# Query features of the last batch one per unit, and two more down chunks in exact parts

## The chip, the cores and the metric

The kernel runs on one core of a Trainium2 chip. The metric is device time in microseconds (us) of one execution. The core has five instruction queues that run side by side and wait for each other by semaphores: TensorE (PE, with its weight loads shown apart as PEld), VectorE (DVE), ScalarE (ACT), GpSimd (POOL) and SyncE (SP, which here only issues DMAs). SBUF is the on-chip memory of the engines, PSUM the memory that TensorE accumulates into[...].

## The reference

Two stages, one after the other: a linear attention with polynomial features, then a gated feed-forward block on its output.

```python
# q, k, v: (4, 4, 1088, 32); S1, S2: (8, 32)
def phi(x):
    a = einsum('rd,bhsd->bhsr', S1, x)
    b = einsum('rd,bhsd->bhsr', S2, x)
    return einsum('bhsi,bhsj->bhsij', a, b).reshape(..., 64)
q_p, k_p = phi(q), phi(k)
kv = einsum('bhsf,bhsd->bhfd', k_p, v)
z = sum(k_p, axis=2)
attn = einsum('bhsf,bhfd->bhsd', q_p, kv) / (einsum('bhsf,bhf->bhs', q_p, z) + 1e-6)

x = attn.transpose(0, 2, 1, 3).reshape(4352, 128)
g = x @ w_gate                       # (128, 1536)
out = (g * sigmoid(g) * (x @ w_val)) @ w_out   # (1536, 128)
```

All inputs and outputs are float32.

## The kernel before

The feed-forward work is cut into token blocks. Three small blocks come from the first batch; then come the *later blocks* (the list `line`), six of 480 tokens and a last one of 384. The hidden dimension of 1536 is cut into 12 chunks of 128. One block and one chunk make a **unit**; the main loop over `y` (the last `for y in range(END)`) runs 7 x 12 = 84 units in order, so the first later block is units 0 to 11, the third one (`line[2]`) units 24 to 35.

A unit works in two halves, and the halves of neighbouring units overlap. In step `y`, `start_unit` of unit y+1 runs first: two matmuls (L990) into the gate bank and the value bank of a pair of PSUM banks, which ScalarE then rescales in place (L993). Then `finish_unit` of unit y adds four matmuls (L1002, L1003). These are float32 products done as three fast products of cut-down operands ("parts"). ScalarE applies Silu to the gate bank into `sg` (L1005), and VectorE multiplies by the value bank into `hbuf` (L1010). There are three pairs of banks, so unit y+3 reuses unit y's pair: its first L990 overwrites the gate bank, read last by L1005, its second L990 the value bank, read last by L1010.

After that comes `down`, the product of a finished chunk with `w_out`. The list `todo` holds five chunks, so the chunk of unit y-5 is taken in step y. It is done in one of two ways. A *plain* chunk is one full float32 matmul (L1078), two instructions in the trace. A chunk in the list `DOWN` is done in *exact parts*: three fast matmuls (L1070, L1072, L1073) on parts of the hidden values, which `cut_hidden` makes for it. The three parts are made by three engines. The first (`h1`) comes one unit later, on ScalarE (L969, put behind the unit's other work in `behind`) or on VectorE (L967, put ahead of it in `before`). The second (`h0 = h - h1`) comes two units later on GpSimd (L970), the third (`hd`) three units later on VectorE (L973). `cut_hidden` rotates over six sets of three buffers. In the third later block the chunks 2, 4, 6, 8, 9 and 10 are in `DOWN`, all six with `h1` on ScalarE; in the fourth, chunks 1, 2, 4, 5, 7, 8, 9, 10, and in the fifth and sixth chunk 6 too, with `h1` of 2, 5, 8 and 10 on VectorE.

Tokens of the next block are cut into parts by `cut_tokens`: first part on ScalarE (L865), second on GpSimd (L868), third on VectorE (L873). For the fourth later block this takes place at units 27 and 32.

Between these units the attention of batches 1 to 3 advances. It is a generator (`attentions`), and `parts_of(n)` takes n steps of it. In units below 20 one step is taken in each unit, from 20 on only in even ones. At the units in `GROUPS` (4, 6, 20, 22, 40) `group` runs it up to the next step that holds many matmuls. Of batch 3, the last, the group at unit 22 makes the query sketches; then come eight steps of `query_step`: the denominators (L741, L744), their reciprocal (L746 to L748), and three times a feature product (L377) and a transposition (L758). After that nothing is left but the group at unit 40, whose numerators (`numerators`, L776) multiply the transposed features by the key-value sums.

Down weights are cut by `cut_down` in units 20 to 29 on ScalarE (L915, L923, L932) and GpSimd (L918, L926).

The order on each engine is written out by hand (the schedule is manual): instructions run on each engine in the order in which these functions emit them, and `now(before, y)` and `now(behind, y)` emit the pieces that were set aside for unit y.

Of the kernel before, what the change touches and what calls it, by code (L numbers as in the profile page):

```python
# [19 lines left out]
def kernel(  # L20
# [796 lines left out]
    def whole(ap):  # L817
        return ap.bitcast(FP32)
# [66 lines left out]

    line = list(range(HEAD, len(blocks)))
    FINE, PLAIN = range(1, NCH - 1), [0, 1, 3, 5, 7, 6, NCH - 1]
    DOWN = [(line[2], j) for j in (2, 4, 6, 8, 9, 10)]
    DOWN += [(i, j) for i in line[3:6] for j in (1, 2, 4, 5, 7, 8, 9, 10)]
    DOWN += [(i, 6) for i in line[4:6]]  # L890
    DOWN += [(LAST, j) for j in (1, 2, 4, 5, 6, 7)]
    down_parts = {}
# [4 lines left out]
    def add_to(where, y, f):  # L897
        where.setdefault(y, []).append(f)

    def now(where, y):  # L900
        for f in where.pop(y, ()):
            f()
# [49 lines left out]
    def cut_hidden(y, i, j):  # L952

        if not h_sets:
            x = []
            for tag in ("kld", "qld", "vld", "kT", "qT"):
                t = const.tile([P, 2, WB], F32R, tag=tag, name="h" + tag, bufs=1)
                x += [t[:, k, :] for k in range(2)]
            t = const.tile([P, 8, WB], F32R, tag="late", name="hlate", bufs=1)
            x += [t[:, k, :] for k in range(8)]  # L960
            h_sets.extend(x[k : k + 3] for k in range(0, 18, 3))
        n = SPLIT if i == LAST else blocks[i][1]
        h_sets.append(h_sets.pop(0))
        h1, h0, hd = h_parts[i, j] = [x[:, 0:n] for x in h_sets[-1]]
        h = hidden[i, j][:, 0:n]
        if j in (2, 5, 8, 10) and i != line[2]:
            add_to(before, y + 1, lambda: nc.vector.tensor_scalar(h1, h, CUT, None, op0=ALU.mult))  # L967
        else:
            add_to(behind, y + 1, lambda: nc.scalar.activation(h1, h, AF.Copy, scale=CUT))  # L969
        add_to(before, y + 2, lambda: nc.gpsimd.tensor_tensor(  # L970
            out=h0, in0=h, in1=whole(h1), op=ALU.subtract
        ))
        add_to(before, y + 3, lambda: nc.vector.scalar_tensor_tensor(  # L973
            out=hd, in0=whole(h1), scalar=WHOLE, in1=h, op0=ALU.mult, op1=ALU.subtract
        ))
# [8 lines left out]
    def start_unit(i, j):  # L984

        n = blocks[i][1]
        xd = x_parts[i][2][:, 0:n]
        ps = sums_of[i, j] = pair((i, j))[:, :, 0:n]
        for k, w in enumerate((wg, wv)):
            nc.tensor.matmul(  # L990
                ps[:, k], w_parts[id(w), j // 3][2][:, j % 3, :], xd, start=True, stop=True
            )
        nc.scalar.activation(ps, ps, AF.Copy, scale=-1.0 / WHOLE)  # L993

    def finish_unit(i, j, y=None):
        n = blocks[i][1]
        x1, x0, _ = (x[:, 0:n] for x in x_parts[i])
        ps = sums_of.pop((i, j))
        now(before, y)
        for k, w in enumerate((wg, wv)):  # L1000
            w1, wb = (w_parts[id(w), j // 3][t][:, j % 3, :] for t in range(2))
            nc.tensor.matmul(ps[:, k], w1, x1, start=False, stop=False, skip_group_check=True)  # L1002
            nc.tensor.matmul(ps[:, k], wb, x0, start=False, stop=True, skip_group_check=True)  # L1003
        sg = fpool.tile([P, WB], FP32, tag="sg", name="sg", bufs=5)[:, 0:n]
        nc.scalar.activation(sg, ps[:, 0], AF.Silu, scale=WHOLE)  # L1005
        slot_of[i, j] = slots.pop(0)
        hj = slot_of[i, j]
        hidden[i, j] = hj
        todo.append((i, j))
        nc.vector.scalar_tensor_tensor(  # L1010
            out=hj[:, 0:n], in0=ps[:, 1], scalar=WHOLE, in1=sg, op0=ALU.mult, op1=ALU.mult
        )
        let_go((i, j))
        now(behind, y)
        if (i, j) in DOWN:
            cut_hidden(y, i, j)
# [38 lines left out]
    def down(y=None):  # L1055

        i, j = todo.pop(0)
        n = SPLIT if i == LAST else blocks[i][1]
        first = i not in acc
        if first:  # L1060
            acc[i] = bank("g2" if i == 1 or i in line[2::2] else "acc")
        made[i] = made.get(i, 0) + 1
        mine = [c for c in range(NCH) if (i, c) in DOWN]
        if mine and j == mine[0]:
            acc[i, "p"] = bank("acc" if i in line[2::2] else "g2")
        sides = dict(start=first, stop=(made[i] == NCH))
        if j in mine:
            w1, wb, wd = [down_parts[x][:, FINE.index(j), :] for x in ("w1", "wb", "wd")]
            h1, h0, hd = h_parts.pop((i, j))
            nc.tensor.matmul(acc[i][:, 0:n], wd, hd, **sides)  # L1070
            p = acc[i, "p"][:, 0:n]
            nc.tensor.matmul(p, w1, h1, start=(j == mine[0]), stop=False)  # L1072
            nc.tensor.matmul(p, wb, h0, start=False, stop=(j == mine[-1]))  # L1073
            if j == mine[-1]:
                copy_out(y, i, n)
        else:
            w = down_parts["scaled"][:, PLAIN.index(j), :] if mine else wo[:, j, :]
            nc.tensor.matmul(acc[i][:, 0:n], w, hidden[i, j][:, 0:n], **sides)  # L1078
        if i != LAST:
            hidden.pop((i, j))  # L1080
            slots.append(slot_of[i, j])
        if made[i] == NCH:
            if mine:
                put_together(y, i, n)
            elif i == HEAD - 1:

                add_to(behind, 1, lambda: store(i, n))
            else:
                store(i, n)
# [163 lines left out]
    def parts_of(n):  # L1253

        for _ in range(n):
            if ahead[0] not in ("pe", "end"):
                ahead[0] = next(att, "end")

    def group():
        while ahead[0] != "pe":  # L1260
            ahead[0] = next(att)
        ahead[0] = next(att, "end")
# [132 lines left out]
    slots[:] = [flat[:, WB * k : WB * k + WB] for k in range((NH - NL) * BW // WB)]  # L1395

    END = len(line) * NCH
    GROUPS, WIDE, EASY = (4, 6, 20, 22, 40), (20, 40), 20

    token_steps = {}  # L1400
    for m, i in enumerate(line[1:], 1):
# [4 lines left out]
    for y in range(END):  # L1406
        if y in GROUPS:
            group()
        at = [(line[x // NCH], x % NCH) for x in (y, y + 1) if x < END]
        if y in WIDE:  # L1410
            finish_unit(*at[0], y)
        if y + 1 < END:
            start_unit(*at[1])
        if y not in WIDE:
            finish_unit(*at[0], y)
        for _ in range(2):

            if len(todo) > min(5 + (todo[0] == (line[1], 0)), END - y + 1):
                down(y)
        parts_of(y < EASY or y % 2 == 0)  # L1420
        for gen in token_steps.get(y, ()):
            next(gen, None)
        if y in range(20, 30):
            next(down_steps, None)
# [43 lines left out]
```

## Time and profile before

| | us |
|---|---|
| median of three runs | 276.89 |
| lowest and highest | 276.75, 277.1 |
| the profiled execution | 276.78 |
| its span, first to last instruction | 275.0 |

Busy time in four stretches of the span (us; the first holds units 23 to 28, the next units 29 to 34, then 35 to 39, and the group at unit 40):

| stretch | length | TensorE | VectorE | ScalarE | GpSimd |
|---|---|---|---|---|---|
| 145.7 to 158.4 | 12.70 | 12.70 | 7.97 | 11.35 | 4.69 |
| 158.4 to 170.8 | 12.40 | 12.40 | 8.99 | 11.05 | 5.35 |
| 170.8 to 180.9 | 10.10 | 10.10 | 8.30 | 8.66 | 4.11 |
| 180.9 to 184.8 | 3.90 | 3.82 | 2.24 | 1.61 | 2.01 |

The profile names engines and lines: "DVE L1010" is the VectorE instruction of line 1010. In the timeline each line has the start in us from the span's beginning, the duration, engine, line, operation, output and input names with their shapes, a count, and in brackets how long the engine had stood idle and whom it waited for. The granted TensorE clock was 1.000 throughout. A matmul's duration in the trace includes its time in the pipeline, so the pace of TensorE is read from the distance between starts.

### The profile page before, as it was taken

To read this page: it belongs to the slowest core of one execution; us is meant where nothing else is said; L and a number is where in the kernel's file an instruction comes from. 1 tells how busy PE (TensorE), PEld (TensorE's weight loads), DVE (VectorE), ACT (ScalarE), POOL (GpSimd) and SP (SyncE) were. 2 spreads that over 40 slices of the span, in tenths; PEclk is the share of its full clock that TensorE was granted. 3 is DMA by queue.
4 is the path that set the end of the run, shared out by engine and by line. 5 is a ranking of instruction groups with operands and counts; after the bars stand their busy time and mean duration, and the time that the engine had idled before them with its cause. 6 is when DMAs were issued, how large, how long until landed. Compare 5 with 4: busy or idle time off the path is not lost.

```text
span 275.0 us, 5775 instructions
## 1 busy us (share of the span) xinstructions
PE 269.2 (98%) x2189; PEld 200.3 (73%) x2189; DVE 212.5 (77%) x371; ACT 192.8 (70%) x347; POOL 103.5 (38%) x115
## 2 busy tenths in 40 slices
PE   8899999999999999999999999999999999999995
PEld 7545566666785787777577777867887888789994
DVE  3997988989798773887545666967977996998771
ACT  3468565472685686677479898769879888897880
POOL 3314422159250630260043353435335663553320
PEclk9999999999999999999999999999999999999999
DMA  6583196222231043000200020000100200010021
GB/s 192 170 228 83 43 278 190 68 97 70 54 92 21 1 115 95 2 0 0 38 13 4 4 36 0 0 2 11 26 2 0 36 1 0 14 24 1 5 33 29
DMA packets 26139, 14.30 MB, mean 52 GB/s; under 512 B 19840, under 2 KB 24192, under 8 KB 26112
## 3 DMA queue, kind: packets, MB, share of 16 engines
q1 hardware_dynamic: 25456, 13.84, 19.6%
q8 instruction: 17, 0.28, 0.4%
q10 hardware_dynamic: 656, 0.10, 0.2%
q14 instruction: 10, 0.08, 0.1%
HBM read 11.41 MB, written 2.23 MB: 50 GB/s over the span
## 4 chain that ended last, share of the span: by engine, by line
PE 93%; DVE 3%; DMA 2%; ACT 1%; issue 0%; SPq 0%
PE PS L1078 21%; PE PS L1002 14%; PE PS L990 14%; PE PS L1003 14%; PE PS L1026 12%; PE PS L1070 3%; PE PS L1073 3%; PE PS L1072 3%; PE PS L354 2%; PE PS L776 2%; PE PS L342 2%; PE PS L388 2%; DMA kld<-in_k_dram 2%; PE PS L1118 1%; PE PS L497 1%; PE PS L445 1%
## 5 line engine op out<-in xcount | busy, mean ns | idle before, releaser
L993 ACT ACTIVATE PS<-PS 128x960 f32<-128x960 f32 (+1 forms) x90 | 83.3, 926 | 30.6 <-PE PS L990 29.8
L1010 DVE SCALAR_TENSOR_TENSOR hbuf<-PS,sg 128x480 f32<-128x480 f32 (+1 forms) x87 | 55.2, 635 | 38.4 <-ACT sg L1005 35.4
L1005 ACT ACTIVATE sg<-PS 128x480 f32<-128x480 f32 (+1 forms) x90 | 49.6, 551 | 1.6 <-PE PS L1003 1.2
L1078 PE MATMUL PS<-hbuf,wo 128*128 128x480 f32 (+2 forms) x94 | 39.4, 516 | 0.0
L990 PE MATMUL PS<-xd,graw 128*128 128x480 f32 (+1 forms) x69 | 37.7, 546 | 0.0
L990 PE MATMUL PS<-xd,wd 128*128 128x480 f32 (+1 forms) x90 | 33.5, 372 | 0.0
L1003 PE MATMUL PS<-x,wb 128*128 128x480 f32 (+1 forms) x90 | 33.5, 372 | 0.0
L1002 PE MATMUL PS<-x,w 128*128 128x480 f32 (+1 forms) x90 | 33.4, 371 | 0.0
L1003 PE MATMUL PS<-x,graw 128*128 128x480 f32 (+1 forms) x69 | 25.5, 370 | 0.0
L990 PEld LDWEIGHTS PS<-xd,wd 128*128 128x128 f32 x90 | 17.0, 189 | 10.0 <-issue 5.5
L1026 PE MATMUL PS<-xT,wg 128*128 128x384 f32 (+1 forms) x60 | 23.5, 474 | 0.1
L1026 PE MATMUL PS<-xT,wv 128*128 128x384 f32 (+1 forms) x60 | 23.1, 467 | 0.3 <-DVE wv L286 0.3
L1078 PEld LDWEIGHTS PS<-hbuf,wo 128*128 128x128 f32 x94 | 17.6, 189 | 5.4 <-issue 0.4
L868 POOL TENSOR_TENSOR x<-xT,x 128x480 fp32r<-128x480 f32 (+1 forms) x6 | 7.2, 1193 | 38.0 <-ACT x L865 38.0
L1030 ACT ACTIVATE sg<-PS 128x384 f32<-128x384 f32 (+1 forms) x24 | 11.2, 468 | 13.2 <-PE PS L1026 12.4
L970 POOL TENSOR_TENSOR hlate<-hbuf,hlate 128x480 fp32r<-128x480 f32 (+1 forms) x12 | 14.3, 1188 | 14.2 <-ACT hlate L969 11.3
L1078 PE MATMUL PS<-hbuf,scaled 128*128 128x480 f32 (+1 forms) x44 | 18.7, 514 | 0.0
L990 PEld LDWEIGHTS PS<-xd,graw 128*128 128x128 f32 x69 | 13.0, 188 | 7.7 <-ACT PS L993 4.1
L1002 PEld LDWEIGHTS PS<-x,w 128*128 128x128 f32 x90 | 16.9, 188 | 2.2
L1003 PEld LDWEIGHTS PS<-x,wb 128*128 128x128 f32 x90 | 16.9, 188 | 2.1
L1002 PE MATMUL PS<-x,graw 128*128 128x480 f32 (+1 forms) x48 | 18.0, 376 | 0.0
L1026 PEld LDWEIGHTS PS<-xT,wv 128*128 128x128 f32 x60 | 11.2, 190 | 7.4 <-DVE hbuf L1041 0.8
(205 smaller groups left out, 565.1 us busy)
## 6 DMA issues: line engine op xcount, KB each, us to landing
kld<-in_k_dram SPq DMA_DIRECT2D x4, 544.0 KB, 4.2
vld<-in_v_dram SPq DMA_DIRECT2D x12, 144.0 KB, 4.0
qld<-in_q_dram SPq DMA_DIRECT2D x3, 544.0 KB, 4.0
raw<-in_moe_w_out_dram SPq DMA_DIRECT2D x4, 384.0 KB, 4.3
raw<-in_moe_w_gate_dram SPq DMA_DIRECT2D x3, 384.0 KB, 3.3
raw<-in_moe_w_val_dram SPq DMA_DIRECT2D x3, 384.0 KB, 3.6
out_dram<-o SPq DMA_DIRECT2D x16, 60.0 KB, 2.0
vld<-in_v_dram SPq DMA_DIRECT2D x4, 112.0 KB, 3.9
```

The lines of the kernel that those rows point to most:

```text
L970: add_to(before, y + 2, lambda: nc.gpsimd.tensor_tensor(out=h0, in0=h, in1=whole(h1), op=ALU.subtract))
L990: nc.tensor.matmul(ps[:, k], w_parts[id(w), j // 3][2][:, j % 3, :], xd, start=True, stop=True)
L993: nc.scalar.activation(ps, ps, AF.Copy, scale=-1.0 / WHOLE)
L1002: nc.tensor.matmul(ps[:, k], w1, x1, start=False, stop=False, skip_group_check=True)
L1003: nc.tensor.matmul(ps[:, k], wb, x0, start=False, stop=True, skip_group_check=True)
L1005: nc.scalar.activation(sg, ps[:, 0], AF.Silu, scale=WHOLE)
L1010: nc.vector.scalar_tensor_tensor(out=hj[:, 0:n], in0=ps[:, 1], scalar=WHOLE, in1=sg, op0=ALU.mult, op1=ALU.mult)
L1026: nc.tensor.matmul(o[:, 0:n], w[:, j, :], xT[:, t0 : t0 + n], start=True, stop=True)
L1030: nc.scalar.activation(sg[:, 0:n], g[:, 0:n], AF.Silu)
L1070: nc.tensor.matmul(acc[i][:, 0:n], wd, hd, **sides)
L1072: nc.tensor.matmul(p, w1, h1, start=(j == mine[0]), stop=False)
L1078: nc.tensor.matmul(acc[i][:, 0:n], w, hidden[i, j][:, 0:n], **sides)
```

## The change

It has three edits. The attention takes a step in every unit from 24 to 31 (`SOON`), where it took one in even units only. The last batch's six feature steps, which were in the even units 26 to 36, are then in units 25 to 30, one in each. In the third later block chunks 5 and 7 join `DOWN`: their down products are made of exact parts and no longer of one plain matmul, and their three parts are made by the engines named above. And in that block `h1` of chunks 5, 7 and 9 is on VectorE; chunks 2, 4, 6, 8 and 10 have it on ScalarE.

On VectorE this adds three L967 and two L973, on GpSimd two L970; ScalarE has one L969 less; on TensorE two L1078 matmuls are replaced by two each of L1070, L1072 and L1073. SP's list is the same.

```diff
@@
     line = list(range(HEAD, len(blocks)))
     FINE, PLAIN = range(1, NCH - 1), [0, 1, 3, 5, 7, 6, NCH - 1]
-    DOWN = [(line[2], j) for j in (2, 4, 6, 8, 9, 10)]
+    DOWN = [(line[2], j) for j in (2, 4, 5, 6, 7, 8, 9, 10)]
     DOWN += [(i, j) for i in line[3:6] for j in (1, 2, 4, 5, 7, 8, 9, 10)]
@@
         h = hidden[i, j][:, 0:n]
-        if j in (2, 5, 8, 10) and i != line[2]:
+        if j in ((5, 7, 9) if i == line[2] else (2, 5, 8, 10)):
             add_to(before, y + 1, lambda: nc.vector.tensor_scalar(h1, h, CUT, None, op0=ALU.mult))
         else:
             add_to(behind, y + 1, lambda: nc.scalar.activation(h1, h, AF.Copy, scale=CUT))
@@
     END = len(line) * NCH
-    GROUPS, WIDE, EASY = (4, 6, 20, 22, 40), (20, 40), 20
+    GROUPS, WIDE, EASY, SOON = (4, 6, 20, 22, 40), (20, 40), 20, range(24, 32)
@@
             if len(todo) > min(5 + (todo[0] == (line[1], 0)), END - y + 1):
                 down(y)
-        parts_of(y < EASY or y % 2 == 0)
+        parts_of(y < EASY or y % 2 == 0 or y in SOON)
         for gen in token_steps.get(y, ()):
             next(gen, None)
```

## The prediction

> **What bounds the kernel now.** I read the page's busy shares and its chain of waits, then the timeline around units 24 to 40, then who waits for whom.
>
> ```profile
> PE 269.2 (98%) x2189; PEld 200.3 (73%) x2189; DVE 212.5 (77%) x371; ACT 192.8 (70%) x347; POOL 103.5 (38%) x115
> PE 93%; DVE 3%; DMA 2%; ACT 1%; issue 0%; SPq 0%
> PEld PS L990 <- DVE hbuf L1010: 1.2, 5, 0.4
> ```
>
> TensorE carries 93% of the chain; VectorE holds TensorE up (third line: products of L990 waiting for L1010) for 1.2 us in the whole run. So matmul time saved reaches the end, unless another engine becomes late. The cadence is the distance between the last matmuls (L1003) of successive units:
>
> ```profile
> 162.62 0.38 PE L1003 MATMUL PS<-x,wb 128*128 128x480 f32 x1
> 162.84 0.97 PE L1078 MATMUL PS<-hbuf,scaled 128*128 128x480 f32 x2
> ...
> 164.74 0.38 PE L1003 MATMUL PS<-x,wb 128*128 128x480 f32 x1
> 164.96 0.39 PE L1070 MATMUL PS<-hqld,dparts 128*128 128x480 f32 x1
> ...
> 166.70 0.38 PE L1003 MATMUL PS<-x,wb 128*128 128x480 f32 x1
> ```
>
> A unit with a plain down chunk (L1078) takes 2.12, one with a chunk in parts (L1070, L1072, L1073) 1.96. Call t(y) the start of unit y's last L1003: t(30) is 162.62, t(31) 164.74, t(32) 166.70, t(33) 168.82, t(34) 170.76. A down chunk runs five units after its own, so chunks 5 and 7 of the third later block (units 29 and 31) run after t(34) and t(36).
>
> What VectorE does meanwhile, and how it meets GpSimd:
>
> ```profile
> 162.17 0.62 DVE L973 SCALAR_TENSOR_TENSOR hqld<-hkld,hbuf 128x480 fp32r<-128x480 f32 x1
> 162.41 1.46 POOL L970 TENSOR_TENSOR hvld<-hbuf,hqld 128x480 fp32r<-128x480 f32 x1 [1.71 <-ACT hqld L969]
> 162.71 0.65 DVE L1010 SCALAR_TENSOR_TENSOR hbuf<-PS,sg 128x480 f32<-128x480 f32 x1
> 163.72 0.66 DVE L1010 SCALAR_TENSOR_TENSOR hbuf<-PS,sg 128x480 f32<-128x480 f32 x1 [0.36 <-ACT sg L1005]
> ...
> 172.32 1.22 POOL L970 TENSOR_TENSOR hlate<-hbuf,hlate 128x480 fp32r<-128x480 f32 x1 [0.68 <-ACT hlate L969]
> 172.36 2.00 DVE L377 TENSOR_TENSOR phq<-qab 128x768 f32<-128x768 f32 x1
> ```
>
> L970 takes 1.22 and L377 0.95 alone. At 172.36 L377 took 2.00: it ended 0.82 after L970. At 162.41 L970 was the second and took 1.46. L1010 (one operand in PSUM) keeps 0.65. Two arrivals close together look like this:
>
> ```profile
> 208.84 1.22 POOL L970 TENSOR_TENSOR hkT<-hbuf,hkT 128x480 fp32r<-128x480 f32 x1
> 209.53 1.05 DVE L873 SCALAR_TENSOR_TENSOR xd<-x,xT 128x480 fp32r<-128x480 f32 x1
> 210.03 1.63 POOL L970 TENSOR_TENSOR hlate<-hbuf,hqT 128x480 fp32r<-128x480 f32 x1
> 210.50 1.67 DVE L973 SCALAR_TENSOR_TENSOR hqT<-hkT,hbuf 128x480 fp32r<-128x480 f32 x1
> 212.10 0.65 DVE L1010 SCALAR_TENSOR_TENSOR hbuf<-PS,sg 128x480 f32<-128x480 f32 x1
> ```
>
> They alternate: the one that waits goes next, a blocked L873 or L973 ends 0.51 after the L970 ahead of it, a blocked L970 1.08 after its blocker. This L1010 came 1.6 after its gate values (sg) were there, and the unit still took 2.14: that is about all the lateness TensorE forgives. L1010(y) frees the value bank that the second L990 of unit y+3 overwrites; that product starts about t(y+1) + 1.1.
>
> **What the Trainium skill says.** SBUF — State Buffer, "Who interferes with whom": VectorE with two SBUF inputs, or in a 2-port mode, and a GpSimd instruction that reads SBUF shut each other out for a whole instruction; with one SBUF input there is no contention. The lines above agree (2.00 for 0.95; L1010 unmoved; a transpose, L578, kept 0.69 beside L868 at 98.97). VectorE: DVE Perf Modes, "The perf-mode tier table": tensor_scalar on fp32 in SBUF runs at 2x, two-input operations at 1x. Here L967 has 0.40 as its undisturbed median, L973 0.61 to 0.65. Perfetto Trace Analysis, "GPSIMD Engine Instruction", calls GpSimd spans unreliable; I use the ends only where a VectorE instruction confirms them.
>
> **The change, part by part.**
>
> TensorE: two plain chunks become parts: 2 x (2.12 - 1.96) = **-0.32**. ScalarE: six L969 become five (-0.61), which has cover both before and after. GpSimd: two more L970, 2 x 1.22, no deadline near (three units ahead of the product). VectorE: three L967 (3 x 0.40) and two more L973 (2 x 0.61) = +2.4. The moved steps issue no DMA, and SP's list is unchanged; the third pair of L377 and L758 comes at units 29 and 30 (before: 34 and 36), the first two at 25 to 28. The first two fit: L377 at unit 25 meets GpSimd's L926 (153.61 to 154.89), so L1010(26) starts at 155.6, half a microsecond late, which TensorE forgives; unit 27's L377 only delays GpSimd; by unit 28 all is as before.
>
> Units 29 to 33 are where the additions pile up. VectorE is in order, so I lay its list end to end (about 0.08 of each duration overlaps the next):
>
> - L377 (unit 29) starts behind L1010(29), at 163.28; the L970 of chunk 4 holds the port until 163.87: ends 164.69. The new L967 of chunk 5: to 165.0. L1010(30): 164.93 to 165.58 (before 163.72 to 164.38). Its bank is due at 165.6. No stall, but the cover is gone.
> - L758 to 166.45, L973 of chunk 4 at 166.36. GpSimd's L970 of chunk 5 runs 165.15 to 166.37, and the next, chunk 6, is ready at about 166.33 (L969 needs L1010(30), 165.64 to 166.25). This is a tie.
> - **A, VectorE first:** L973(4) to 166.98, L1010(31) to 167.55, in time. L973(5) waits for L970(6), to 168.5. L967(7) to 168.8, L1010(32) 168.75 to 169.4. L873 waits for L970(7) (168.96 to 170.18), to 170.68. L970(8), ready at 170.36, goes next, to 171.75; L973(6) to 172.25. L1010(33) 172.2 to 172.85. The second L990 of unit 36 was due at 171.85 and starts at 173.1: **+1.25**.
> - **B, GpSimd first:** L973(4) ends 168.07, L1010(31) 168.64. The second L990 of unit 34 moves from 167.94 to 168.92: **+0.98**. After that the same collisions fall where TensorE is a microsecond later, and L1010(33), ending 172.47, is just in time.
>
> Afterwards VectorE has L973 (1.40 when blocked) plus L1010 (0.57) a unit, which fits 1.96, and from unit 37 no L970 is in the way: lag gone, the loss stays. TensorE's wait before L776 at unit 40 (0.85) cannot absorb it: it hangs on unit 39's own sg and L1010, which move along.
>
> Sum on the profiled execution, 276.78 (span 275.0 and 1.78 around it): A -0.32 + 1.25 = +0.93, 277.71; B -0.32 + 0.98 = +0.66, 277.44. The runs' median is 276.89, so add 0.11 for a median: 277.82 and 277.55. I take **277.7**, between them, since the tie is within 0.05. Either lag may be off by 0.3 either way (the bounds are the exact lock times), so the case itself spans 277.2 to 278.1.
>
> **Rivals.**
>
> 1. Not slower: no stall. The fifth later block has seven chunks in a row in parts, three L967 among them, and TensorE keeps 1.96 (221.78 to 233.54). Then only the saving counts: 276.89 - 0.32 = 276.57. This decides if L377 of unit 29 slips in ahead of the L970, or L1010 has more than the 1.6 of forgiveness. Against it: that block has no L377 and L758 in it, and its L873 at 233.45 had only a partly used lag behind it.
> 2. Both ties go to GpSimd: B's 0.98, and L973(6) behind L970(8) as well, about 1.0 more: 276.89 - 0.32 + 1.98 = 278.55. For it: at 172.32 the GpSimd start was 0.04 ahead and won. Against: in B L973(6) starts ahead by some 0.06.
> 3. Something faster than counted, a wait in front of L776 at unit 40 shortened by the features being ready at unit 30 instead of 36: up to 0.85, 275.7. Against it: there TensorE waits for L1010, not for L758.
>
> **How the numbers follow.** Forecast 0.57, rival 1 0.26, rival 2 0.13, rival 3 0.04. The 276.5 to 278.6 range leaves out rival 3 and the tails. A measurement of this kernel tells about 0.2% (0.55) from no change, so slower starts at 277.44. Of the forecast some 0.53 lies above it, with rival 2 0.66; rival 1 and the rest of the forecast make 0.30 the same; faster 0.04.
>
> **What would show it.** Right: in the new timeline two matmul cadences of 1.96 where 2.12 stood (after t(34) and t(36)), an L377 of about 1.4 at unit 29, an L1010(30) near 164.93, and one gap of 0.9 to 1.3 before a second L990 of unit 34 or 36, put down to DVE hbuf L1010. Wrong: no such gap (then rival 1), or a gap at another unit, or one on ScalarE. It also fails if blocked L973 in units 31 to 33 show 0.65 instead of 1.1 to 1.7.

## The result, and the profile after

| | before | changed |
|---|---|---|
| median of 21 runs, us | 277.01 | 277.76 |
| lowest and highest | 276.64, 278.42 | 277.46, 278.23 |
| the profiled execution | 276.78 | 277.96 |
| its span | 275.0 | 276.2 |

The ratio of changed to before is 1.0022, with a 95% interval of 1.0013 to 1.0031: slower by 0.36 to 0.86 us. Two of the 21 runs of before (278.29 and 278.42) stand almost 1 us above the other nineteen; no trace of such a run is there to say why, and the medians do not depend on them.

On the page after the change, the first two lines answer to those shown of before; the third below is the group of the second product of a unit's start, which had 0.0 of idle time before:

```profile
PE 269.2 (97%) x2191; PEld 200.7 (73%) x2191; DVE 217.4 (79%) x376; ACT 192.3 (70%) x346; POOL 106.7 (39%) x117
PE 87%; DVE 6%; DMA 2%; ACT 2%; issue 1%; SPq 1%; DVEq 0%
L990 PE MATMUL PS<-xd,wd 128*128 128x480 f32 (+1 forms) x90 | 33.6, 374 | 1.0 <-DVE hbuf L1010 1.0
```

In the answer on who waits for whom:

```profile
PEld PS L990 <- DVE hbuf L1010: 2.8, 7, 1.4
```

TensorE is as busy as before in microseconds, but only 87% of the chain is now its own, and VectorE has 6% instead of 3%. The wait of L990 for L1010 has grown from 1.2 to 2.8 us, and one single wait is 1.4 long. It can be seen where it lies in TensorE's timeline (start, duration, line; the bracket is idle time and its releaser):

```profile
171.13 0.38 PE L1003 MATMUL PS<-x,wb 128*128 128x480 f32 x1
171.34 0.38 PE L1070 MATMUL PS<-hqT,dparts 128*128 128x480 f32 x1
171.56 0.38 PE L1072 MATMUL PS<-hkT,dparts 128*128 128x480 f32 x1
171.78 0.38 PE L1073 MATMUL PS<-hkT,dparts 128*128 128x480 f32 x1
171.99 0.37 PE L990 MATMUL PS<-xd,gphq 128*128 128x480 f32 x1
173.34 0.48 PE L990 MATMUL PS<-xd,wd 128*128 128x480 f32 x1 [0.97 <-DVE hbuf L1010]
...
174.31 0.38 PE L1003 MATMUL PS<-x,wb 128*128 128x480 f32 x1
```

The first line is the last L1003 of unit 34. Then comes chunk 5, now in exact parts at 0.22 each: this is the saving. The two L990 start unit 36, and the second stands 1.35 after the first instead of 0.22. From L1003 to L1003 it is 3.18, where 1.95 is the pace with parts: 1.23 lost.

Why that L990 is late is in the timelines of VectorE and GpSimd, put together in order of time (units 29 to 33; this trace runs 0.37 later than that of before at t(30), 162.99 against 162.62):

```profile
162.78 1.47 POOL L970 TENSOR_TENSOR hvld<-hbuf,hqld 128x480 fp32r<-128x480 f32 x1 [1.36 <-ACT hqld L969]
163.64 1.42 DVE L377 TENSOR_TENSOR phq<-qab 128x768 f32<-128x768 f32 x1
164.98 0.40 DVE L967 TENSOR_SCALAR hkT<-hbuf 128x480 fp32r<-128x480 f32 x1
165.30 0.65 DVE L1010 SCALAR_TENSOR_TENSOR hbuf<-PS,sg 128x480 f32<-128x480 f32 x1
...
166.73 1.73 POOL L970 TENSOR_TENSOR hlate<-hbuf,hqT 128x480 fp32r<-128x480 f32 x1
166.76 0.61 DVE L973 SCALAR_TENSOR_TENSOR hvld<-hqld,hbuf 128x480 fp32r<-128x480 f32 x1
167.29 0.64 DVE L1010 SCALAR_TENSOR_TENSOR hbuf<-PS,sg 128x480 f32<-128x480 f32 x1
...
169.37 2.83 POOL L970 TENSOR_TENSOR hlate<-hbuf,hlate 128x480 fp32r<-128x480 f32 x2 [0.92 <-DVE hlate L967]
169.78 1.33 DVE L873 SCALAR_TENSOR_TENSOR xd<-x,xT 128x480 fp32r<-128x480 f32 x1
171.04 1.68 DVE L973 SCALAR_TENSOR_TENSOR hlate<-hqT,hbuf 128x480 fp32r<-128x480 f32 x1
172.64 0.64 DVE L1010 SCALAR_TENSOR_TENSOR hbuf<-PS,sg 128x480 f32<-128x480 f32 x1
```

Read it from below. The last L1010 is unit 33's. Its sg had been ready since 170.16 (L1005 of that unit starts at 169.59 and takes 0.57), so it starts 2.5 late and ends at 173.28; the second L990 of unit 36, due at about 171.85 + 0.37 = 172.2, starts 0.06 after that end. Ahead of it stands the L973 of chunk 6, 1.68 where it takes 0.65 alone; ahead of that L873, 1.33 for 0.61. Both lie across the two L970 of 2.83 (chunks 7 and 8). At the top is where the lag begins: L377 at unit 29 behind the L970 of chunk 4. In before the same instructions of units 32 and 33 (L873, the L973 of chunk 6, the L1010 of unit 33) come ahead of the next L970, and none is lengthened:

```profile
169.18 0.61 DVE L873 SCALAR_TENSOR_TENSOR xd<-x,xT 128x480 fp32r<-128x480 f32 x1
169.71 0.65 DVE L973 SCALAR_TENSOR_TENSOR hqT<-hkT,hbuf 128x480 fp32r<-128x480 f32 x1
170.28 0.65 DVE L1010 SCALAR_TENSOR_TENSOR hbuf<-PS,sg 128x480 f32<-128x480 f32 x1
170.43 1.22 POOL L970 TENSOR_TENSOR hlate<-hbuf,hqT 128x480 fp32r<-128x480 f32 x1 [2.94 <-ACT hqT L969]
```

Not all of the 2.5 is lost. The L990 starts 1.13 after it was due (173.34 against 172.21), so about 1.35 was forgiven, less than the 1.6 that the prediction read off a unit with plain chunks. By estimate the difference comes of the down chunks in that stretch: both are in parts here (chunk 4 already in before, chunk 5 by the change), and each brings that L990 forward by 0.16 (2.12 less 1.96).

### The profile page after: what moved, and what is told of

Read it like the earlier page. It is cut to its first block, busy times and chain, and to the rows that moved or that the text cites. A ratio compares the mean times of both kernels' runs of the same rounds, so it can differ in the third digit from the quotient of the medians.

```text
span 276.2 us, 5789 instructions
## 1 busy us (share of the span) xinstructions
PE 269.2 (97%) x2191; PEld 200.7 (73%) x2191; DVE 217.4 (79%) x376; ACT 192.3 (70%) x346; POOL 106.7 (39%) x117
## 4 chain that ended last, share of the span: by engine, by line
PE 87%; DVE 6%; DMA 2%; ACT 2%; issue 1%; SPq 1%; DVEq 0%
PE PS L1078 19%; PE PS L1002 13%; PE PS L990 13%; PE PS L1003 13%; PE PS L1026 12%; PE PS L1073 3%; PE PS L1070 3%; PE PS L1072 3%; PE PS L354 2%; PE PS L776 2%; PE PS L342 2%; DMA kld<-in_k_dram 2%; PE PS L388 2%; PE PS L1118 1%; DVE hbuf L1010 1%
## 5 line engine op out<-in xcount | busy, mean ns | idle before, releaser
L993 ACT ACTIVATE PS<-PS 128x960 f32<-128x960 f32 (+1 forms) x90 | 83.3, 926 | 32.0 <-PE PS L990 31.2
L1010 DVE SCALAR_TENSOR_TENSOR hbuf<-PS,sg 128x480 f32<-128x480 f32 (+1 forms) x87 | 55.2, 634 | 34.3 <-ACT sg L1005 32.2
L1005 ACT ACTIVATE sg<-PS 128x480 f32<-128x480 f32 (+1 forms) x90 | 49.6, 552 | 1.6 <-PE PS L1003 1.3
L1078 PE MATMUL PS<-hbuf,wo 128*128 128x480 f32 (+2 forms) x94 | 39.4, 516 | 0.0
L990 PE MATMUL PS<-xd,graw 128*128 128x480 f32 (+1 forms) x69 | 37.6, 546 | 0.0
L990 PE MATMUL PS<-xd,wd 128*128 128x480 f32 (+1 forms) x90 | 33.6, 374 | 1.0 <-DVE hbuf L1010 1.0
L1003 PE MATMUL PS<-x,wb 128*128 128x480 f32 (+1 forms) x90 | 33.5, 372 | 0.0
L1002 PE MATMUL PS<-x,w 128*128 128x480 f32 (+1 forms) x90 | 33.4, 371 | 0.0
L1003 PE MATMUL PS<-x,graw 128*128 128x480 f32 (+1 forms) x69 | 25.5, 370 | 0.0
L990 PEld LDWEIGHTS PS<-xd,wd 128*128 128x128 f32 x90 | 17.0, 189 | 11.0 <-issue 4.7
L1078 PEld LDWEIGHTS PS<-hbuf,wo 128*128 128x128 f32 x94 | 17.6, 189 | 5.4 <-issue 0.4
L990 PEld LDWEIGHTS PS<-xd,graw 128*128 128x128 f32 x69 | 13.0, 188 | 7.7 <-ACT PS L993 4.1
L1002 PEld LDWEIGHTS PS<-x,w 128*128 128x128 f32 x90 | 16.9, 187 | 2.2
L1003 PEld LDWEIGHTS PS<-x,wb 128*128 128x128 f32 x90 | 16.9, 188 | 2.1
L1002 PE MATMUL PS<-x,graw 128*128 128x480 f32 (+1 forms) x48 | 18.0, 375 | 0.0
L970 POOL TENSOR_TENSOR hlate<-hbuf,hlate 128x480 fp32r<-128x480 f32 (+1 forms) x12 | 14.3, 1198 | 8.9 <-ACT hlate L969 5.5
L1078 PE MATMUL PS<-hbuf,scaled 128*128 128x480 f32 (+1 forms) x40 | 16.8, 508 | 0.0
```

The lines of the kernel that those rows point to most:

```text
L970: add_to(before, y + 2, lambda: nc.gpsimd.tensor_tensor(out=h0, in0=h, in1=whole(h1), op=ALU.subtract))
L990: nc.tensor.matmul(ps[:, k], w_parts[id(w), j // 3][2][:, j % 3, :], xd, start=True, stop=True)
L1010: nc.vector.scalar_tensor_tensor(out=hj[:, 0:n], in0=ps[:, 1], scalar=WHOLE, in1=sg, op0=ALU.mult, op1=ALU.mult)
```

## The experiments

Seven more kernels were run. "The port" is the path to SBUF that VectorE and GpSimd share, in the prediction's sense; an instruction is "blocked" where it takes longer because the other engine holds it. "Unit" figures are distances between last L1003, as before.

**e1: the feature steps alone.** The kernel before with only the moved feature steps of the change.

```diff
-    GROUPS, WIDE, EASY = (4, 6, 20, 22, 40), (20, 40), 20
+    GROUPS, WIDE, EASY, SOON = (4, 6, 20, 22, 40), (20, 40), 20, range(24, 32)
...
-        parts_of(y < EASY or y % 2 == 0)
+        parts_of(y < EASY or y % 2 == 0 or y in SOON)
```

> Only the feature steps of the last batch are moved to units 24 to 31; the chunks in exact parts and the engines of their first parts are as before. Theory (VectorE falls behind in units 29 to 33 because the new parts come on top of the moved steps, on a port that it shares with GpSimd): the third L377 at unit 29 is still blocked to about 1.4, but without L967 and two of the L973 the lag is gone at unit 31; no gap before a second L990, units at 2.12 and 1.96 as before, time within 0.3 us of before. Rival (the moved steps alone make VectorE late): a gap of about 1 us in units 32 to 36, some 0.9 us slower than before.

Measured: median 276.86, ratio to before 0.9995 (0.9980 to 1.0011), span 275.0 as before. No unit from t(27) on is more than 0.01 longer than before: 1.96, 2.12, 1.95, 2.09, 1.95 after t(31), and L990 waits 1.2 for L1010, as before. The moved steps cost nothing by themselves, although the third L377 is blocked here too, as VectorE's timeline of e1 shows:

```profile
163.31 1.42 DVE L377 TENSOR_TENSOR phq<-qab 128x768 f32<-128x768 f32 x1
164.65 0.65 DVE L1010 SCALAR_TENSOR_TENSOR hbuf<-PS,sg 128x480 f32<-128x480 f32 x1
...
167.74 0.66 DVE L1010 SCALAR_TENSOR_TENSOR hbuf<-PS,sg 128x480 f32<-128x480 f32 x1 [0.45 <-ACT sg L1005]
```

By unit 32 (last line) VectorE again waits for ScalarE, not the other way round: the lag has gone, one unit later than expected (the L1010 of unit 31, at 166.65, still starts about 0.9 late).

**e2: the parts alone.** The changed kernel with the feature steps left in even units.

```diff
-    GROUPS, WIDE, EASY, SOON = (4, 6, 20, 22, 40), (20, 40), 20, range(24, 32)
+    GROUPS, WIDE, EASY, SOON = (4, 6, 20, 22, 40), (20, 40), 20, ()
```

> Chunks 5 and 7 in exact parts and L967 for 5, 7, 9 as in the change, but the feature steps stay in even units (26 to 36). Theory (shared port, VectorE in order): the steps at units 30, 32, 34 now fall among the parts, and one gap becomes two, of about 1.2 each (second L990 of units 36 and 38): 1.2 slower than the changed kernel, 2.1 slower than before. Rival 1 (the moved steps cause the loss): no gap, the saving of 0.32 shows, 276.7. Rival 2 (the parts alone cause it, the features do not matter): the same 1.2 gap as the changed kernel, about 277.8.

Measured: median 279.26 of six runs, ratio 1.0078 (1.0050 to 1.0105): 2.36 slower than before, where 2.1 was expected. From t(30) to the first L776 of unit 40 the trace has 21.47 against 19.20, so 2.27. There are two long units, 3.19 after t(34) and 3.29 after t(36), in front of the second L990 of units 36 and 38. The second one in TensorE's timeline of e2, and in those of VectorE and GpSimd together:

```profile
177.32 0.38 PE L990 MATMUL PS<-xd,gphq 128*128 128x480 f32 x1
178.76 0.48 PE L990 MATMUL PS<-xd,wd 128*128 128x480 f32 x1 [1.05 <-DVE hbuf L1010]
```

```profile
174.82 1.71 DVE L377 TENSOR_TENSOR phq<-qab 128x768 f32<-128x768 f32 x1
176.03 1.59 POOL L970 TENSOR_TENSOR hvld<-hbuf,hqld 128x480 fp32r<-128x480 f32 x1 [0.32 <-ACT hqld L969]
176.45 1.69 DVE L973 SCALAR_TENSOR_TENSOR hlate<-hlate,hbuf 128x480 fp32r<-128x480 f32 x1
178.06 0.64 DVE L1010 SCALAR_TENSOR_TENSOR hbuf<-PS,sg 128x480 f32<-128x480 f32 x1
```

It is again an L377 that is blocked and then an L973 behind the next L970. So it is not the moving of the steps that costs: with the steps in their old units the same parts cost a gap more, and moving them removes about half of the loss. With e1 and e4 (below) this says that the loss needs both, the added parts and feature steps among them.

**e3: two GpSimd instructions exchanged.** The changed kernel; TensorE, VectorE, ScalarE and SP have the same lists.

```diff
-        add_to(before, y + 2, lambda: nc.gpsimd.tensor_tensor(
+        add_to(*((behind, y + 3) if (i, j) == (line[2], 8) else (before, y + 2)), lambda: nc.gpsimd.tensor_tensor(
```

> The changed kernel with two GpSimd instructions exchanged: L970 of chunk 8 after that of chunk 9. Every other engine has the same list. Theory (the gap comes from L970 of chunk 8 taking the shared port between L873 and L973 of chunk 6): L970 of 9 has to wait for its L967, so L973 of chunk 6 finds the port free and takes 0.6 instead of 1.68; L1010 of unit 33 comes about 1.1 earlier, and the gap of 1.23 shrinks to about 0.2: some 1.0 faster than the changed kernel, 0.1 faster than before. Rival (VectorE simply has too much to do in units 29 to 33, whoever holds the port): the gap stays near 1.2, time as the changed kernel.

Measured: median 276.68, ratio to before 0.9986 (0.9977 to 0.9994). The unit after t(34) takes 2.13 instead of 3.18: a gap of 0.18 is left. VectorE and GpSimd of e3 in order of time:

```profile
169.21 1.22 POOL L970 TENSOR_TENSOR hlate<-hbuf,hlate 128x480 fp32r<-128x480 f32 x1 [0.92 <-DVE hlate L967]
169.63 1.33 DVE L873 SCALAR_TENSOR_TENSOR xd<-x,xT 128x480 fp32r<-128x480 f32 x1
170.88 0.65 DVE L973 SCALAR_TENSOR_TENSOR hlate<-hqT,hbuf 128x480 fp32r<-128x480 f32 x1
171.45 0.64 DVE L1010 SCALAR_TENSOR_TENSOR hbuf<-PS,sg 128x480 f32<-128x480 f32 x1
...
173.12 1.24 POOL L970 TENSOR_TENSOR hkld<-hbuf,hkld 128x480 fp32r<-128x480 f32 x1 [2.68 <-PE PS L1003]
```

L873 is still blocked (1.33), but the L973 behind it takes 0.65, since the next L970, that of chunk 9, does not come before 173.12. VectorE has exactly the work and the order that it has in the changed kernel. That it has too much to do in these units, whoever holds the port, is thereby refuted. The median is 0.22 below before; 0.1 was expected.

**e4: the feature steps one unit earlier.**

```diff
-    GROUPS, WIDE, EASY, SOON = (4, 6, 20, 22, 40), (20, 40), 20, range(24, 32)
+    GROUPS, WIDE, EASY, SOON = (4, 6, 20, 22, 40), (20, 40), 20, range(23, 31)
```

> The changed kernel with the feature steps in units 23 to 30, one unit earlier. Theory (the lag begins where the third L377 at unit 29 waits for L970 of chunk 4): at unit 28 that L377 finds the port free, 0.95 instead of 1.42; L1010 of unit 30 comes about 0.4 earlier and the cover is not used up; after that L873 and L973 of chunk 6 go ahead of L970 of chunk 8, and there is no gap above 0.2: only the saving of 0.32 stays, about 276.7 beside 277.0 before. Rival (too much work on VectorE in units 29 to 33 in any case): a gap of 0.8 or more in units 34 to 36 stays, 277.3 or more.

Measured: median 276.53, ratio 0.9983 (0.9974 to 0.9993). All units from t(33) to t(39) take 1.94 to 1.97: no gap, and both savings are there. This is faster than both kernels, by 0.19 to 0.72 us against before. VectorE and GpSimd of e4 at units 28 and 33:

```profile
161.52 0.92 DVE L377 TENSOR_TENSOR phq<-qab 128x768 f32<-128x768 f32 x1
162.36 0.65 DVE L973 SCALAR_TENSOR_TENSOR hqld<-hkld,hbuf 128x480 fp32r<-128x480 f32 x1
162.62 1.47 POOL L970 TENSOR_TENSOR hvld<-hbuf,hqld 128x480 fp32r<-128x480 f32 x1 [1.71 <-ACT hqld L969]
...
170.34 0.65 DVE L973 SCALAR_TENSOR_TENSOR hlate<-hqT,hbuf 128x480 fp32r<-128x480 f32 x1
170.57 1.51 POOL L970 TENSOR_TENSOR hlate<-hbuf,hlate 128x480 fp32r<-128x480 f32 x1 [0.67 <-ACT hlate L969]
```

The third L377 finds the port free (0.92 instead of 1.42), and nine microseconds on the L973 of chunk 6 comes 0.23 ahead of the L970 of chunk 8 and not behind it. Now GpSimd waits, which costs nothing. The edit moves all six steps, so the last L758 has left unit 30 as well (it stands at 163.49, ahead of the L1010 of unit 30); e4 does not tell the half microsecond of the L377 from this.

**e5: L873 at unit 27 instead of 32.**

```diff
-        for at in {1: (3, 8), 2: (20, 21), 3: (27, 32), 4: (40, 42)}.get(m, (NCH * m - 10, NCH * m - 9)):
+        for at in {1: (3, 8), 2: (20, 21), 3: (27, 27), 4: (40, 42)}.get(m, (NCH * m - 10, NCH * m - 9)):
```

> The changed kernel with L873 (third part of the fourth block's tokens) on VectorE at unit 27 instead of unit 32. The work of every engine is the same in kind and number, only this one instruction stands earlier. Theory (L873 waits a full L970 at unit 32 and then lets L970 of chunk 8 in ahead of L973 of chunk 6): L873 at unit 27 is blocked behind L868 (about 1.6) and delays nothing that matters; L1010 of unit 33 comes about 1 us earlier, gap 1.23 becomes 0 to 0.2, about 276.7. Rival (the third L377 at unit 29 alone decides, L873 does not matter): a gap of 0.8 or more stays, 277.4.

Measured: median 276.72, ratio 0.9992 (0.9986 to 0.9999). L873 takes 1.66 at 158.91 and delays nothing; the L973 of chunk 6 is blocked by one L970 only (1.33), and the unit after t(34) takes 1.95. A small gap of 0.07 is left after t(31) (2.03). The third L377 is blocked here as in the changed kernel (1.41), so that alone does not make the gap: it takes L873 in unit 32 as well.

**e6: all first parts of the block on ScalarE.**

```diff
-        if j in ((5, 7, 9) if i == line[2] else (2, 5, 8, 10)):
+        if j in (() if i == line[2] else (2, 5, 8, 10)):
```

> The changed kernel with all eight first parts of the third later block on ScalarE (L969), none on VectorE (three L967 less there). Theory: VectorE wins 3 x 0.32 in units 30 to 34 and L970 of chunk 5 no longer waits for VectorE, so L973 of chunk 6 goes before L970 of chunk 8 and there is no gap; ScalarE needs 0.87 + 0.45 + 0.61 = 1.93 a unit, which just fits 1.96: about 276.6. Rival (ScalarE becomes the bound, which is what the L967 are there for): units 33 to 36 take 2.0 to 2.2 instead of 1.96, or a wait of L1002 for L993 of 0.5 or more in all, 277.1 or more.

Measured: median 276.69, ratio 0.9994 (0.9980 to 1.0007); the interval doesn't tell it from before, so that it is faster is not shown. But the trace has no gap: units of 1.94 to 1.97 from t(33) on, and the wait of L1002 for ScalarE's L993 is 1.5 in all, as before. (So the sign named above, 0.5 or more in all, was there already and decides nothing; the length of the units does.) ScalarE goes from the L969 of chunk 9 (172.06, 0.61) straight into the L993 of unit 36 (172.68), and that unit still keeps 1.97. The third L377 and L873 are blocked here too (1.42 and 1.21). So the L967 are part of the cause, and ScalarE had room for these first parts.

**e7: steps one unit earlier and chunk 3 in exact parts too.**

```diff
-    DOWN = [(line[2], j) for j in (2, 4, 5, 6, 7, 8, 9, 10)]
+    DOWN = [(line[2], j) for j in (2, 3, 4, 5, 6, 7, 8, 9, 10)]
```

(with e4's edit)

> Feature steps in units 23 to 30, and chunk 3 of the third later block in exact parts as well, its first part on ScalarE. It asks how much further the same trade goes. The saving is another 0.16 (2.12 to 1.96 after unit 32). Theory: ScalarE has no idle time at units 27 to 29 (L865 and L932 lie there), so the new L969 at unit 28 makes L1002 of unit 30 wait about 0.3 for L993; and one more L970 and L973 at units 29 and 30 put VectorE a blocked 0.8 later, so a gap before a second L990 in units 32 to 36 comes back, 0.3 to 1.2: slower than the kernel with the steps one unit earlier by 0.4 to 1.3. Rival (room is left): 276.4.

Measured: median 278.3, ratio 1.0043 (1.0030 to 1.0057). From t(29) to t(36) it takes 1.66 more than e4 (15.84 against 14.18), above the 0.4 to 1.3 that was expected. There are two gaps where one was expected: 2.33 instead of 1.96 after t(31) (and 2.20 instead of 2.11 after t(30)), and 3.28 instead of 1.95 after t(34), the second in the place of the changed kernel and with the same look in the timelines of VectorE and GpSimd of e7:

```profile
170.12 1.33 DVE L873 SCALAR_TENSOR_TENSOR xd<-x,xT 128x480 fp32r<-128x480 f32 x1
170.97 1.56 POOL L970 TENSOR_TENSOR hkld<-hbuf,hkld 128x480 fp32r<-128x480 f32 x1
171.38 1.67 DVE L973 SCALAR_TENSOR_TENSOR hlate<-hlate,hbuf 128x480 fp32r<-128x480 f32 x1
172.97 0.65 DVE L1010 SCALAR_TENSOR_TENSOR hbuf<-PS,sg 128x480 f32<-128x480 f32 x1
```

ScalarE's share is small: the weight loads of L1002 wait 1.7 for L993 in all, 0.4 more than in e4, but the unit in which ScalarE is late, after t(29), takes 2.15 against 2.13. Both gaps are before a second L990 that waits for L1010. With the steps and engines as they stand here, one more chunk is too much for VectorE beside GpSimd; other places for it were not tried.

## Why the prediction was right

**The saving.** The two units, 2.12 each before, are predicted to save 0.32. In e4, where nothing covers it, they take 1.95 and 1.95 (after t(34) and t(36)), 0.15 and 0.17 less than before's 2.10 and 2.12. Right, 0.32.

**Where the lag begins.** With 0.37 taken off, the changed kernel's L377 ends at 164.69 and L1010 of unit 30 starts at 164.93, both to the hundredth as worked out; it did not stall TensorE (2.12 after t(32)). e4 and e5 add that the steps in these units are needed for the loss but not enough: with them a unit earlier (e4), or with L873 away (e5), the end of the chain fails to form.

**The tie, and case A.** GpSimd's L970 starts at 166.73 and VectorE's L973 at 166.76, but L973 takes 0.61 and L970 1.73: VectorE went first. So the case that happened is A, with its one gap at unit 36: 1.25 worked out, 1.23 measured. The way there holds as well: L873 to 170.68 (170.74), L973 of chunk 6 to 172.25 (172.35), L1010 of unit 33 to 172.85 (172.91). The agreement of the two totals is in part luck: the working lets L990 start 0.25 after that end, in the trace it is 0.06, so that L990 is 1.13 late and not 1.25; but the L1002 after it stands 0.32 behind it and not 0.22, which the working had not counted. One reason for rival 2 fell: an earlier start in the profile doesn't show who gets the port. At 172.36 in the trace of before the L970 that started 0.04 ahead won, here the one that started 0.03 ahead lost. There GpSimd had stood idle for 0.68, here its L970 followed directly on another that ended at 166.70; the prediction did not use that difference. From 60 us on, the traces of all nine kernels have 21 places where an L970 starts 0.03 to 0.12 ahead of one of VectorE's L377 or L973. In 18 of them GpSimd had been idle for 0.67 or more, and the L970 went first; in the three where it followed another L970 within 0.03 (changed kernel, e3, e5) VectorE did. The lead was 0.03 in these three and 0.04 or more in the others, so it could also be the lead that decides; no run was made to separate them. That the tie fell to A was thus not foreseen.

**The sum.** A gives 277.71 for the profiled execution and 277.82 for a median, against 277.96 and 277.76. The 277.7 was put between two cases, and only A came; that it met the median to 0.06 is luck as well. The medians differ by 0.75, and the ratio says 0.36 to 0.86, where A has +0.93, just above that, and B +0.66. The profiled pair differs by 1.18, but 0.37 of that arises before unit 30, and 0.35 before any instruction differs (t(22) is 145.70 before and 146.05 after). Kernels that are alike up to t(30) vary by as much: 162.62 before and 163.15 in e2, 162.66 in e1 and 162.99 in the changed one. From t(30) to the first L776 of unit 40 it is 19.20 before and 20.13 after, A's +0.93; from t(30) to the span's end 112.38 and 113.21, so +0.83. The waits of the weight loads of L776 at unit 40 are 0.33 and 0.56 in both traces: as predicted, they absorb nothing. Whether every timed run falls into A was not seen; a profile shows one.

**The rivals.** Rival 1 (no stall) needed room that isn't there: e3, e4, e5 and e6 come near its time (276.53 to 276.72), each by changing one of the ingredients. Its counterexample, the fifth block, has seven chunks in a row without stall, but no feature steps beside them. Rival 3 had nothing behind it: the steps were ready six units earlier in e1, and nothing was gained.

**The shared port.** The rule of the Trainium skill that was used (SBUF — State Buffer, "Who interferes with whom") says that one of the two is fully blocked while the other's instruction lasts. All of e1 to e7 agree: blocked L973 end 0.5 after the L970 (up to 1.70 for 0.65), and L1010 and the L758 keep 0.64 to 0.66 and 0.93 to 0.97 in these units. The prediction counted each L967 at 0.40. In the changed kernel that came out, but an L967 can be blocked as well, though it has one input: the first in e2 took 0.76 beside the L970 at 162.94, one of before 1.28 beside the L970 at 180.44.

## What to carry to other kernels

When work is added to an engine that is off the critical path, lay its list end to end over the units concerned, with the instructions of the engine that shares a port with it. A sum over the stretch would have left VectorE time to spare (by estimate: 8.99 us of work in the 12.40 of units 29 to 34 before, and 2.4 more); in the changed trace it is busy without a pause from 163.0 to 174.4, with four instructions blocked there (L377, L873 and two L973). What decided was which of two short instructions came first. And if such a pile-up costs more than the change saves, move the work to other units (e4, e5), or exchange two instructions on the other engine (e3), before giving the change up: e4 turned 0.22% slower into 0.17% faster with the same work.

## What the runs showed that was not expected

Who gets the shared port can't be read from the starts: an L970 that followed another without a pause lost to an L973 that started 0.03 later (changed kernel; in e3 166.59 and 166.62, in e5 166.70 and 166.73, the same way each time). And lags that were each harmless, a third L377 blocked for 0.5 (e5) and a blocked L873 at unit 32 (e4, 1.32), cost 1.23 where both stand together with the L967 and with the L970 of chunk 8 in its place; without one of these two the loss is gone or almost gone (e6, e3). TensorE forgives a late L1010 up to a limit, here 1.35, and waits for the rest: in the changed kernel and in both gaps of e2 the second L990 starts 0.06 after L1010's end.
